# Talking-heads attention and a leaky MLP on one core: raw weight pieces loaded one or two per unit, with four always held

## The chip, the cores and the metric

One core of a Trainium2 chip runs the whole program. The metric is device time in microseconds (us) of one execution; lower is better. Before the change it is 891.46 us (median of 3 runs, 890.16 to 892.83).

## What is computed

```python
# q, k, v: (4, 12, 448, 64); w_pre, w_post: (12, 12)
scores = scale * np.matmul(q, k.transpose(0, 1, 3, 2))
scores = np.einsum('bhij,hg->bgij', scores, w_pre)
attn = np.exp(scores - np.max(scores, axis=-1, keepdims=True))
attn = attn / (np.sum(attn, axis=-1, keepdims=True) + 1e-09)
attn = np.einsum('bhij,hg->bgij', attn, w_post)
x = np.matmul(attn, v)          # then (tokens, 768)
h = x @ w_in                    # w_in: (768, 2048)
g = np.maximum(0.01 * h, h)
out = g @ w_out                 # w_out: (2048, 768)
```

The weights of the MLP arrive as 64-bit numbers, seen as pairs of 32-bit words, and the kernel makes 32-bit floats of them itself.

## The kernel before, in words

**Two phases.** For the first 370 us or so the core computes the attention, for the last 434 us the MLP; some 80 us between them prepare the MLP's operands. The attention is cut into chunks of 120 rows (the last of each batch of 448 has 88), 16 chunks in all, and each chunk `n` into three **units** `s` = 0, 1, 2. A unit has the number `at = 3 * n + s`. The instructions of every engine stand in the order in which the program records them (`pin`, L143), so each engine works through its own list and waits at the first entry that is not ready.

**What a unit does.** For the next unit it mixes the raw scores over the heads: `first` (L218) multiplies the tiles `r` by `kpre` into the PSUM tile `psm`, DVE takes the maxima, ACT the exponentials (`power`, L236, tile `et`). For its own unit it mixes the exponentials back: `mix` (L258), PSUM tile `psa`. `values` (L313, PSUM tile `psx`) multiplies by v for the unit three back. `scores` (L184, PSUM tile `pss`) makes two head pairs of raw scores for the chunk after next, and ACT moves them to the SBUF tile `st` (`move`, L198). `pss`, `psa` and `psx` share a pool of two PSUM buffers (`ps_x`). So an ordinary unit opens on TensorE with a `psm`, and has `psa`, `pss`, `psm`, `pss`, `psa`, `psx` behind it.

**The tiles r.** They are re-reads of `st` in another layout, by DMA: `refill` (L208) issues them on SyncE's queue (SP), four in most units, into a ring of eight tiles, so two units ahead of their use. `st` has two buffers: the first move into a chunk's `st` (the unit with `s` = 0) waits until the DMAs that read the chunk two before have ended.

**The weights.** 48 pieces of the MLP's weights are turned into floats beside the attention, by the class `Narrow` (L74). A piece is loaded raw (L96, `craw`, four buffers, SP's queue), read by ACT into two tiles (`spread`, L102 and L103), put together by DVE (`assemble`) and GpSimd (`join`), and stored to DRAM (L123). The number `count` of pieces that a unit spreads, at its end, is 1, and 2 in the units 5, 11, 17, 23, 29, 35 and 40. The load stands before that, behind the unit's refills:

```python
while len(loaded) < 4 - count and pieces:
    loaded.append(Narrow(p_c, *pieces.pop(0)))
...
for _ in range(count):
    spread()
```

`loaded` holds the pieces that were issued and not yet spread; three are issued ahead of unit 0. Counted out, unit 0 loads none, an ordinary unit one, a unit with `count` = 2 none, and the unit behind it three. All loads of q, k, v (but for some of v), all refills, the raw loads and the stores of pieces share SP's one queue.

Of the kernel before, what the change touches and what calls it, by code (L numbers as in the profile page):

```python
# [34 lines left out]
def kernel(  # L35
# [47 lines left out]
    class Narrow:  # L83
# [14 lines left out]
        def spread(self):  # L98
            self.low, self.high = self.raw[:, :, 0], self.raw[:, :, 1]
            self.w = self.pool.tile([P, PIECE], F32, tag="w", name="w", bufs=self.bufs[1])  # L100
            self.z = self.pool.tile([P, PIECE], F32, tag="z", name="z", bufs=self.bufs[2])
            pin(nc.scalar.activation(self.z, self.high.bitcast(F32), AF.Copy, scale=2.0**-112))  # L102
            pin(nc.scalar.activation(self.w, self.low, AF.Copy, scale=2.0**-52))  # L103

        def assemble(self):
            z = self.z
            self.top = top = self.pool.tile([P, PIECE], U32, tag="top", name="top", bufs=self.bufs[2])
            pin(nc.vector.tensor_scalar(
                top, z.bitcast(U32), 3, 0x7FFFFFF8, op0=ALU.logical_shift_left, op1=ALU.bitwise_and
            ))  # L110
            pin(nc.vector.scalar_tensor_tensor(
                top, z.bitcast(U32), 0x80000000, top, op0=ALU.bitwise_and, op1=ALU.bitwise_or
            ))
            self.exp = z
            pin(nc.vector.tensor_scalar(z.bitcast(U32), top, 0xFF800000, None, op0=ALU.bitwise_and))
# [68 lines left out]
    def scores(n, a, banks=(ps_x, "x")):  # L184
        b, m = chunks[n][0], width(n)
        if a == 0:
            s_t[n] = p_s.tile([CHUNK, H, S], F32, tag="s", name="st")
        pool, tag = banks
        ps = pool.tile([P, 2, 512], F32, tag=tag, name="pss")
        for z in (0, HP):  # L190
            cols = slice(z, min(z + HP, m))
            for e in range(2):
                up = slice(D * e, D * (e + 1))
                mm(ps[cols, e, :S], q_t[n][up, a, cols], k_t[b, a][up], start=True, stop=True)
        return s_t[n][:m, a::NPAIR, :], ps[:m, :, :S]

    def move(to, ps):
        pin(nc.scalar.activation(to, ps, AF.Copy, scale=scale))  # L198
# [9 lines left out]
    def refill(count, *queues):  # L208
        for _, i in zip(range(count), placed):
            n, g = groups[i]  # L210
            m = width(n)
            r_t[n, g] = t = r_all[i % RING]
            pin((queues or (nc.sync, nc.sync))[g % 2].dma_start(  # L213
                t[LOW:LOW + RH], s_t[n][g:m:m // ROWS]
            ))

    def first(n, s, u):

        sg = chunks[n][3][s]
        if u == 0:
            e_t[n, s] = [], p_st.tile([P, 3, NJ], F32, tag="st", name="stat")
        raw = [r_t.pop((n, 2 * sg[u] + b)) for b in range(2)]
        ps = ps_m.tile([P, 2, 512], F32, tag="m", name="psm")
        for b in range(2):
            for y, up in enumerate((slice(0, HP), slice(HP, LOW + RH))):
                mm(ps[HP * b:HP * (b + 1), y, :S], kpre[up], raw[b][up], start=True, stop=True)
        return n, s, u, ps

    def maxima(n, s, u, ps):
        pin(nc.vector.tensor_reduce(  # L232
            e_t[n, s][1][:, 0, 2 * u:2 * u + 2], ps[:, :, :S], axis=AX.X, op=ALU.max, negate=True
        ))

    def power(n, s, u, ps, which=(0, 1)):  # L236
        es, st = e_t[n, s]
        for y in which:
            g = 2 * u + y
            e = p_e.tile([P, S], F32, tag="e", name="et")  # L240
            es.append(e)
            pin(nc.scalar.activation(  # L242
                e, ps[:, y, :S], AF.Exp, bias=st[:, 0, g:g + 1], accum_out=st[:, 1, g:g + 1]
            ))

    def weights(n, s):
        es, st = e_t[n, s]
        kp = p_st.tile([P, NJ, H, ROWS // 2], F32, tag="kp", name="kp")
        kp_t[n, s] = kp
        z = len(es)  # L250
        rs = st[:, 2, :z]
        pin(nc.vector.tensor_scalar_add(rs, st[:, 1, :z], 1e-9))
        pin(nc.vector.reciprocal(rs, rs))
        pin(nc.vector.tensor_mul(
            kp[:, :z].rearrange("p g h x -> p g (h x)"),
            kpost.rearrange("p h x -> p (h x)").unsqueeze(1).broadcast_to([P, z, RH // 2]),
            rs.unsqueeze(2).broadcast_to([P, z, RH // 2]),
        ))  # L258
# [42 lines left out]
    def keep_at(moves):  # L301
        for copy, to, src in moves:
            for_copy(copy, to, src)
# [28 lines left out]
    def keep_x(n, s, ps):  # L332
        m = width(n)
        pin(nc.vector.tensor_copy(  # L334
            xo_t[n][:, RUN * s:RUN * (s + 1), :m].rearrange("p a (x g) -> p a g x", x=ROWS),
            ps[:, :RUN, :m].rearrange("p a (g x) -> p a g x", x=ROWS),
        ))

    def store_x(n):
        b, i0, m, _ = chunks[n]  # L340
        to = x_dram[b][:, NC * i0:NC * (i0 + m)].rearrange("p (c i) -> p c i", c=NC)
        pin(nc.sync.dma_start(to, xo_t.pop(n)[:, :, :m]))
# [220 lines left out]
    def quads_of(n, s):  # L563
        return len(chunks[n][3][s]) if n < NCK else 0
# [13 lines left out]
    pieces = [(f, j) for f in range(NF) for j in range(4)]  # L578
    late_pieces = [(f, j) for f, j in pieces if f >= NF // 2 and j > 1]
    pieces = [piece for piece in pieces if piece not in late_pieces]  # L580
    loaded = [Narrow(p_c, *pieces.pop(0)) for _ in range(3)]
# [28 lines left out]
    def transfers(n, s, c):  # L610
        b = chunks[n][0]
        t = NJ * s + c
        if t == HALF + 1 and n + 3 < NCK:
            load_q(n + 3)
        due = (n % NB - 1) * SLOTS + t - 3
        if b + 1 < B and due % 2 == 0 and 0 <= due < 2 * NPAIR:
            load_k(b + 1, due // 2)
        if n % NB == 0 and n and c == 1 and s:
            load_v(b, s - 1)
        if n % NB == 1 and n > 1 and t == 1:  # L620
            load_v(b, 2)
# [67 lines left out]
    for n in range(NCK):  # L689
        b = chunks[n][0]  # L690
        last = n == NCK - 1
        for s in range(3):
            at = 3 * n + s
            count = (at + 1) * 48 // 41 - at * 48 // 41 if at < 41 else 0
            nxt = (n, s + 1) if s < 2 else (n + 1, 0)
            to, pair = n + 2, 2 * s

            while storing and storing[0][0] < at - (at < 43):
                storing.pop(0)[1].store()
            if at >= 42:  # L700
                end_period(n, s)
                continue

            if kept:
                keep_x(*kept)
            dues = [first(*nxt, 0)] if quads_of(*nxt) else []
            for due in dues:
                maxima(*due)
            refill(2 * len(dues))
            transfers(n, s, 0)  # L710
            if pending:
                keep_at(mix(*pending, 1))
                pending = None
            if to < NCK:
                move(*scores(to, pair))
            transfers(n, s, 1)
            if n > 1 and s == 0:
                store_x(n - 2)
            weights(n, s)

            if quads_of(*nxt) > 1:
                dues.append(first(*nxt, 1))
                maxima(*dues[1])
            if dues:
                power(*dues[0], (0,))
            if to < NCK:
                move(*scores(to, pair + 1))
            refill(2 * len(dues[1:]))
            if dues:
                power(*dues[0], (1,))  # L730
            transfers(n, s, 2)
            while len(loaded) < 4 - count and pieces:
                loaded.append(Narrow(p_c, *pieces.pop(0)))
            keep_at(mix(n, s, 0))
            pending = n, s
            while spreading:
                assemble()
            for due in dues[1:]:
                power(*due)
            for _ in range(count):  # L740
                spread()
            kept = values(n - 1, s) if n else None
            transfers(n, s, 3)
            for piece in joining:
                piece.join()
            storing.extend((at, piece) for piece in joining)
            joining.clear()
# [15 lines left out]
    loaded = []  # L763
# [103 lines left out]
```

## Time and profile before

| what | value |
|---|---|
| median of the runs | 891.46 us |
| time of the profiled execution | 888.53 us |
| its span, first to last instruction | 886.8 us |
| PE matmul busy | 812.8 us (92%) |
| DVE busy | 554.0 us (62%) |
| ACT busy | 510.9 us (58%) |
| GpSimd busy | 137.7 us (16%) |
| mean granted TensorE clock | 0.973 |
| DMA | 150.58 MB, mean 170 GB/s |

The span leaves 1.73 us of the profiled execution's time around it. Busy time is an average over two unlike phases. The MLP keeps TensorE busy nearly without a gap; the attention has gaps on every engine, and what ends them is read from the waits and the timeline of that stretch. The DMA share of a stretch is how busy the 16 DMA engines were in it.

### The profile page before, as it was taken

Reading aid. Unit: us, or ns where it says so; the run is one execution under the profiler, and the core shown is the slowest. Engines: PE = TensorE matmul, PEld = TensorE weight load, DVE = VectorE, ACT = ScalarE, POOL = GpSimd, SP = SyncE. Lnnn points to the kernel's source line nnn. Section 1 sums busy time; section 2 is a strip of 40 time slices with the busy share of each in tenths; the row PEclk is TensorE's granted clock in tenths of the full one; section 3 lists DMA queues with packets and bytes.
Section 4 is the critical chain, followed back from the end, with each engine's and each line's share of the span. In section 5 each row is a group of like instructions: output and inputs, shape, how many; then the busy total and the mean of one; then the engine's idle time right before and its main releaser. Section 6 shows DMA issues by size and latency. Waiting matters only on the chain.

```text
span 886.8 us, 25820 instructions
## 1 busy us (share of the span) xinstructions
PE 812.8 (92%) x10904; PEld 652.2 (74%) x10904; DVE 554.0 (62%) x995; ACT 510.9 (58%) x1000; POOL 137.7 (16%) x161
## 2 busy tenths in 40 slices
PE   8797998978988998958789999999999999999998
PEld 3354665656655665637679999999999999999997
DVE  5477675766857676756876678897645455542443
ACT  3686777756876876744455556574445445443432
POOL 2023245122533225321300000000000000000000
PEclk9899999989999999997999999999999999999999
DMA  6887769776787768563254456526444223221533
GB/s 165 257 256 225 253 200 286 226 227 214 236 257 237 248 208 267 186 198 98 66 186 144 146 152 194 191 87 190 128 124 135 71 72 89 72 72 39 169 109 111
DMA packets 90659, 150.58 MB, mean 170 GB/s; under 512 B 27996, under 2 KB 65584, under 8 KB 90544
## 3 DMA queue, kind: packets, MB, share of 16 engines
q1 hardware_dynamic: 86316, 140.73, 51.5%
q0 software_dynamic: 1680, 4.14, 1.6%
q10 hardware_dynamic: 2548, 4.06, 1.4%
q8 instruction: 86, 1.41, 0.7%
q14 instruction: 29, 0.24, 0.1%
HBM read 85.73 MB, written 23.59 MB: 123 GB/s over the span
## 4 chain that ended last, share of the span: by engine, by line
PE 72%; issue 8%; ACT 7%; DMA 5%; DVE 4%; SPq 2%; POOL 1%; ACTq 0%; POOLq 0%; DVEq 0%
PE pso L148 26%; PE psh L148 22%; PE psx L148 9%; PE psa L148 5%; PE psm L148 5%; PE pss L148 5%; ACT st L198 4%; DMA craw<-in_w_moe 3%; ACT et L242 2%; DVE stat L232 1%; SPq L213 1%; PE idle L148 1%; DMA kt<-in_k 1%; DMA wi<-w_dram 0%; POOL xr L383 0%
## 5 line engine op out<-in xcount | busy, mean ns | idle before, releaser
L148 PEld LDWEIGHTS psa<-kp,et 64*64 64x64 f32 x5888 | 108.6, 140 | 80.9 <-ACT st L198 41.1
L148 PE MATMUL psa<-kp,et 64*64 64x60 f32 (+1 forms) x5888 | 112.4, 224 | 34.2 <-ACT st L198 18.6
L148 PE MATMUL pso<-gh,wl 128*128 128x448 f32 x384 | 140.4, 366 | 0.0
L148 PE MATMUL pso<-gl,wh 128*128 128x448 f32 x384 | 140.3, 365 | 0.0
L148 PE MATMUL pso<-gh,wh 128*128 128x448 f32 x384 | 140.3, 365 | 0.0
L404 DVE TENSOR_TENSOR wl<-wo,wh 128x768 fp32r<-128x768 f32 x64 | 61.2, 956 | 109.0 <-ACT wh L403 108.3
L242 ACT ACTIVATE et<-psm,stat 128x448 f32<-128x448 f32 x184 | 116.1, 640 | 15.7 <-DVE stat L232 15.7
L403 ACT CAST wh<-wo 128x768 fp32r<-128x768 f32 x64 | 53.5, 836 | 121.0 <-PE pso L148 119.8
L232 DVE TENSOR_REDUCE stat<-psm 128x2 f32<-128x896 f32 x92 | 99.5, 1085 | 32.4 <-PE psm L148 32.4
L198 ACT ACTIVATE st<-pss 120x896 f32<-120x896 f32 (+1 forms) x84 | 77.0, 916 | 67.7 <-PE pss L148 52.5
L148 PE MATMUL psm<-r,kpre 64*64 64x448 f32 x736 | 93.7, 567 | 12.3 <-DMA r<-st 9.2
L148 PE MATMUL pss<-kt,qt 64*64 64x448 f32 (+2 forms) x768 | 94.5, 550 | 6.3 <-DMA qt<-in_q 1.8
L119 POOL TENSOR_TENSOR w<-w,z 128x384 f32<-128x384 f32 x48 | 47.9, 999 | 232.3 <-ACT et L242 154.0
L148 PE MATMUL psx<-at,vt 128*64 128x120 f32 (+1 forms) x1152 | 74.4, 282 | 9.6 <-issue 3.5
L148 PEld LDWEIGHTS pso<-gh,wl 128*128 128x128 f32 x384 | 72.1, 188 | 6.4 <-DVE o L519 0.3
L148 PEld LDWEIGHTS pso<-gh,wh 128*128 128x128 f32 x384 | 72.1, 188 | 5.7
L148 PEld LDWEIGHTS pso<-gl,wh 128*128 128x128 f32 x384 | 72.1, 188 | 5.6
L334 DVE COPY xo<-psx 128x240 f32<-128x240 f32 (+1 forms) x48 | 27.2, 568 | 77.4 <-PE psx L148 75.5
L148 PEld LDWEIGHTS psx<-at,vt 128*64 128x64 f32 x1152 | 63.1, 148 | 16.6 <-ACT st L198 9.8
L148 PEld LDWEIGHTS psm<-r,kpre 64*64 64x64 f32 x736 | 25.7, 136 | 40.1 <-issue 26.3
L148 PEld LDWEIGHTS pss<-kt,qt 64*56 64x56 f32 (+2 forms) x768 | 25.1, 129 | 37.7 <-PE pss L148 20.1
L102 ACT ACTIVATE z<-craw 128x384 f32<-128x384 f32 x64 | 36.6, 572 | 23.8 <-DMA craw<-in_w_moe 23.5
(101 smaller groups left out, 1433.6 us busy)
## 6 DMA issues: line engine op xcount, KB each, us to landing
r<-st SPq DMA_DIRECT2D x182, 210.0 KB
craw<-in_w_moe SPq DMA_DIRECT2D x64, 384.0 KB
wo<-w_dram SPq DMA_DIRECT2D x64, 384.0 KB
wi<-w_dram SPq DMA_DIRECT2D x34, 384.0 KB
w_dram<-w SPq DMA_DIRECT2D x64, 192.0 KB
kt<-in_k SPq DMA_DIRECT2D x42, 112.0 KB
x_dram<-xo SPq DMA_DIRECT2D x12, 360.0 KB
xr<-x_dram SPq DMA_DIRECT2D x24, 180.0 KB
```

Source lines behind the costliest of these rows:

```text
L102: pin(nc.scalar.activation(self.z, self.high.bitcast(F32), AF.Copy, scale=2.0**-112))
L119: pin(self.joiner.tensor_mul(w, w, self.exp))
L148: pin(nc.tensor.matmul(*args, **kw))
L198: pin(nc.scalar.activation(to, ps, AF.Copy, scale=scale))
L213: pin((queues or (nc.sync, nc.sync))[g % 2].dma_start(t[LOW:LOW + RH], s_t[n][g:m:m // ROWS]))
L232: pin(nc.vector.tensor_reduce(e_t[n, s][1][:, 0, 2 * u:2 * u + 2], ps[:, :, :S], axis=AX.X, op=ALU.max, negate=True))
L242: pin(nc.scalar.activation(e, ps[:, y, :S], AF.Exp, bias=st[:, 0, g:g + 1], accum_out=st[:, 1, g:g + 1]))
L334: pin(nc.vector.tensor_copy(xo_t[n][:, RUN * s:RUN * (s + 1), :m].rearrange("p a (x g) -> p a g x", x=ROWS), ps[:, :RUN, :m].rearrange("p ...
L403: hold(nc.scalar.copy(hi, raw))
L404: hold(nc.vector.tensor_sub(lo, raw, hi.bitcast(F32)))
```

## The change: what it does

```diff
             transfers(n, s, 2)
-            while len(loaded) < 4 - count and pieces:
+            while len(loaded) < 4 and pieces:
                 loaded.append(Narrow(p_c, *pieces.pop(0)))
             keep_at(mix(n, s, 0))
```

The limit no longer depends on `count`. Unit 0 now loads one piece, a unit with `count` = 2 one, the unit behind it two, and all others one as before. So the first piece of each group of three is issued one unit earlier. The same 64 pieces are loaded, spread and stored. The lists of PE, DVE and ACT keep their order, as does GpSimd's; SP's list is the one that moves.

On SP's list, unit 5 (from its second pair of refills) to unit 6 (its raw loads), before:

```order
L213 DMA r_120<-st 120x1x448
L213 DMA r_121<-st 120x1x448
L156 DMA kt<-in_k 64x448 x2
L123 DMA w_dram_60<-w 128x384
L213 DMA r_122<-st 120x1x448
L213 DMA r_123<-st 120x1x448
L156 DMA kt<-in_k 64x448 x2
L342 DMA x_dram_76<-xo 128x720
L213 DMA r_124<-st 120x1x448
L213 DMA r_125<-st 120x1x448
L96 DMA craw<-in_w_moe 128x768 x3
L123 DMA w_dram_61<-w 128x384
```

and now:

```order
L213 DMA r_120<-st 120x1x448
L213 DMA r_121<-st 120x1x448
L96 DMA craw<-in_w_moe 128x768
L156 DMA kt<-in_k 64x448 x2
L123 DMA w_dram_60<-w 128x384
L213 DMA r_122<-st 120x1x448
L213 DMA r_123<-st 120x1x448
L156 DMA kt<-in_k 64x448 x2
L342 DMA x_dram_76<-xo 128x720
L213 DMA r_124<-st 120x1x448
L213 DMA r_125<-st 120x1x448
L96 DMA craw<-in_w_moe 128x768 x2
```

One raw load has moved from unit 6 into unit 5, ahead of two loads of k, a store and four refills.

On SP's list, units 11 and 12, where a new batch begins, before:

```order
L213 DMA r_118<-st 120x1x448
L213 DMA r_119<-st 120x1x448
L123 DMA w_dram_62<-w 128x384
L213 DMA r_120<-st 120x1x448
L213 DMA r_121<-st 120x1x448
L342 DMA x_dram_76<-xo 128x720
L213 DMA r_122<-st 120x1x448
L213 DMA r_123<-st 120x1x448
L96 DMA craw<-in_w_moe 128x768 x3
```

and now:

```order
L213 DMA r_118<-st 120x1x448
L213 DMA r_119<-st 120x1x448
L96 DMA craw<-in_w_moe 128x768
L123 DMA w_dram_62<-w 128x384
L213 DMA r_120<-st 120x1x448
L213 DMA r_121<-st 120x1x448
L342 DMA x_dram_76<-xo 128x720
L213 DMA r_122<-st 120x1x448
L213 DMA r_123<-st 120x1x448
L96 DMA craw<-in_w_moe 128x768 x2
```

The same move: one of unit 12's three loads stands in unit 11.

On SP's list, units 0 and 1, before:

```order
L213 DMA r_124<-st 120x1x448
L213 DMA r_125<-st 120x1x448
L213 DMA r_118<-st 120x1x448
L213 DMA r_119<-st 120x1x448
L213 DMA r_120<-st 120x1x448
L213 DMA r_121<-st 120x1x448
L96 DMA craw<-in_w_moe 128x768
L167 DMA qt<-in_q 64x6x88 x2
```

and now:

```order
L213 DMA r_124<-st 120x1x448
L213 DMA r_125<-st 120x1x448
L96 DMA craw<-in_w_moe 128x768
L213 DMA r_118<-st 120x1x448
L213 DMA r_119<-st 120x1x448
L213 DMA r_120<-st 120x1x448
L213 DMA r_121<-st 120x1x448
L96 DMA craw<-in_w_moe 128x768
L167 DMA qt<-in_q 64x6x88 x2
```

Unit 0 has a load of its own, ahead of unit 1's four refills and of the loads of q.

## Rows read from the trace of the kernel before

**Rows 1.** Waits, 56 to 374 us: engine, line waited for: us total, times, longest.
```profile
ACT z L102 <- DMA craw<-in_w_moe: 23.4, 6, 6.0
...
ACT st L198 <- DMA r<-st: 4.2, 1, 4.2
```

**Rows 2.** ACT's timeline: start, us, instruction, then [idle before <-what ended it].
```profile
85.75 0.54 ACT L102 ACTIVATE z<-craw 128x384 f32<-128x384 f32 x1 [5.40 <-DMA craw<-in_w_moe]
...
186.32 0.54 ACT L102 ACTIVATE z<-craw 128x384 f32<-128x384 f32 x1 [6.01 <-DMA craw<-in_w_moe]
...
234.48 0.57 ACT L102 ACTIVATE z<-craw 128x384 f32<-128x384 f32 x1 [2.37 <-DMA craw<-in_w_moe]
...
287.59 0.54 ACT L102 ACTIVATE z<-craw 128x384 f32<-128x384 f32 x1 [5.31 <-DMA craw<-in_w_moe]
```

**Rows 3.** SP's timeline, unit 6: the three raw loads.
```profile
80.88 3.40 SPq L96 DMA_DIRECT2D craw<-in_w_moe  x3
```

**Rows 4.** TensorE's timeline: the psm that opens a unit, in five places.
```profile
79.70 0.98 PE L148 MATMUL psm<-r,kpre 64*64 64x448 f32 x8
...
92.26 0.98 PE L148 MATMUL psm<-r,kpre 64*64 64x448 f32 x8
...
99.48 0.98 PE L148 MATMUL psm<-r,kpre 64*64 64x448 f32 x8
...
179.66 0.98 PE L148 MATMUL psm<-r,kpre 64*64 64x448 f32 x8
...
193.72 0.98 PE L148 MATMUL psm<-r,kpre 64*64 64x448 f32 x8
...
231.25 0.98 PE L148 MATMUL psm<-r,kpre 64*64 64x448 f32 x8
...
239.56 0.98 PE L148 MATMUL psm<-r,kpre 64*64 64x448 f32 x8
...
281.63 0.98 PE L148 MATMUL psm<-r,kpre 64*64 64x448 f32 x8
...
293.93 0.98 PE L148 MATMUL psm<-r,kpre 64*64 64x448 f32 x8
```

**Rows 5.** Windows, last columns: granted clock (1.00 is full), DMA share, GB/s.
```profile
116.00:124.00 8.00, 7.44 (x136) 4.86 (x132) 5.67 (x13) 6.57 (x15) 2.00 (x2) 1.00 0.37 138
...
240.00:248.00 8.00, 6.02 (x178) 4.32 (x171) 5.10 (x11) 6.76 (x17) 4.37 (x6) 1.00 1.00 273
...
0.00:374.00 374.00, 326.85 (x7706) 213.23 (x7708) 247.90 (x494) 264.20 (x568) 120.06 (x147) 0.96 0.76 233
```

**Rows 6.** DMA issues of the page: count, KB each.
```profile
craw<-in_w_moe SPq DMA_DIRECT2D x64, 384.0 KB
```

**Rows 7.** TensorE's timeline: idle that nothing in the profile explains ("issue").
```profile
135.33 0.44 PE L148 MATMUL psa<-kp,et 64*64 64x60 f32 x11 [1.09 <-issue]
...
248.25 0.83 PE L148 MATMUL psx<-at,vt 128*64 128x100 f32 x6 [2.14 <-issue]
...
346.78 0.60 PE L148 MATMUL psa<-kp,et 64*64 64x60 f32 x19 [3.38 <-issue]
```

**Rows 8.** Timelines of SP and ACT: unit 8's first refills, unit 9's first move.
```profile
93.84 1.79 SPq L213 DMA_DIRECT2D r<-st  x2
...
102.22 0.92 ACT L198 ACTIVATE st<-pss 120x896 f32<-120x896 f32 x1 [1.17 <-PE pss L148]
```

**Rows 9.** The chain that ended last: start, us, what.
```profile
43.54 3.63 DMA qt<-in_q
...
148.10 2.42 DMA r<-st
```

**Rows 10.** Timelines of ACT and SP, unit 10: spread's end, refills, raw load.
```profile
107.67 0.58 ACT L103 ACTIVATE w<-craw 128x384 f32<-128x384 uint32 x1
...
107.72 1.68 SPq L213 DMA_DIRECT2D r<-st  x2
109.49 0.93 SPq L96 DMA_DIRECT2D craw<-in_w_moe  x1
```

## The prediction

> **What bounds the kernel now.** I read the waits of the attention phase first, because the change touches that phase alone. One wait there names the raw loads: ACT stood idle 23.4 us, six times, until a raw piece had landed [rows 1]. The reader is to see that it is six long waits and not forty short ones. ACT's timeline says where they are [rows 2]: three of 5.40, 6.01 and 5.31 us, and three short ones that make up the rest, 23.4 - 16.7 = 6.7 us. The first stands at the end of unit 6. SP's timeline shows why [rows 3]: the three raw loads of unit 6 begin to be issued at 80.88 us, ACT finishes its other work of the unit at 85.75 - 5.40 = 80.35 us and wants the first of the three at once; it gets it at 85.75 us, 4.9 us after issue. Unit 5 has spread two pieces and loaded none, so unit 6 spreads a piece that it has loaded itself. The same holds behind each unit with `count` = 2, which gives units 6, 12, 18, 24, 30 and 36: six, as the waits say. (Behind unit 40 nothing is left to load.)
>
> The next question is whether ACT's wait is a wait of the kernel. I measure units by the `psm` that opens them on TensorE [rows 4]. An undisturbed unit is 99.48 - 92.26 = 7.22 us. The unit in which ACT waits is 92.26 - 79.70 = 12.56 us, the other two of the long kind 14.06 and 12.30 us. So the path pays: TensorE needs a PSUM buffer that ACT's move of `pss` frees, and that move stands behind the waiting spread in ACT's list. A short wait, at 234.48 us, costs the unit around it 239.56 - 231.25 = 8.31 us, 1.09 us more than an ordinary one.
>
> Last I read the DMA engines, since what is loaded earlier has to find room [rows 5]. Over the attention phase they are busy 0.76 of the time at 233 GB/s. That mean hides both extremes: from 116 to 124 us, where unit 11 runs, the share is 0.37, and from 240 to 248 us, some two units behind a start of a batch, it is 1.00 at 273 GB/s.
>
> **The change, part by part.** Nothing is added or removed; six loads move one unit ahead, and unit 0 gets one. What it does follows from the lists: the piece that unit 6 spreads is loaded in unit 4, two units (14 us) ahead instead of 4.9 us too late.
>
> *The waits removed.* The three long units give 5.34 + 6.84 + 5.08 = 17.3 us over 7.22. For the three short ones the bounds are 0 and ACT's 6.7 us; I take the one pair measured for all three, 3 x 1.1 = 3.3 us. Together **-20.6 us**, at most the 23.4 us that ACT waited.
>
> *What is late next.* Behind a long wait, SP's queue profits from the pause today. In unit 8 the first two refills end their issue at 95.63 us [rows 8], and they are the last reads of a chunk whose buffer unit 9's first move overwrites, at 102.22 us: 6.6 us of room. SP's own work ahead of them is the same number of transfers after the change, while TensorE and ACT come 5.3 us earlier; 1.3 us of room is left. A refill on the chain of waits took 2.42 us from issue to landing [rows 9], so 1.1 us is missing, and with DMA fuller I count 1.7 us. Three times that is 5 us given back. Behind the short waits I take a third of the 3.3 us, 1 us. The bounds are 0 and 10 us, the latter if half of every wait returns; I take **+6 us**.
>
> *The loads moved out of busy stretches.* At the starts of batches (units 12, 24, 36) one load of 384 KB [rows 6] leaves the stretch in which the DMA engines are full and goes into one at 0.37. At 273 GB/s that is 393 KB / 273 = 1.4 us of DMA time, three times 4.3 us. Bounds: 0, and the stalls seen in these stretches: 4.2 us in which a move waited for a refill [rows 1], and 1.09 + 2.14 + 3.38 = 6.6 us in which TensorE stood in the middle of a call with nothing to wait for [rows 7], 10.8 us together. I take **-3 us**, near the 4.3.
>
> The nearest thing to a rule is in the Trainium skill, "Runtime: NRT & Kernel Launch", section "Instruction fetch mechanics": instructions are streamed in blocks by DMA, and the fetch is hidden because a sequencer issues more slowly than the fetch fills. By that, idle inside a call would not come from full DMA engines, the stalls of rows 7 would stay, and the sum would be about 1 to 2 us smaller. The trace has idle of 3.38 us inside one call of 64 alike matmuls, and such idle is longest just where the DMA share is about 1, which speaks for a connection, but does not show it.
>
> *Unit 0's load.* It stands ahead of unit 1's refills and of a load of q that is on the chain of waits for 3.63 us [rows 9]. It costs its issue (0.93 us for one, rows 10) and 1.4 us of DMA time, if both fall on the path: 0 to +2.3 us. I take **+1 us**.
>
> *The loads moved ahead of k.* In units 5, 17 and 29 the raw load now stands ahead of two loads of k and four refills, and delays their issue by up to 0.93 us. The refills are used two units (14 us) later, this k in unit 8. Cost 0; without that cover it is 3 x 0.9 = 2.8 us, which is inside the range.
>
> *Sum.* -20.6 + 6 - 3 + 1 = -16.6 us against the profiled execution's 888.53 us (span 886.8 us), which makes 871.9 us. That execution lies 2.9 us below the median of the runs, so against the median of 891.46 us it is 874.9 us. I predict **875 us**. The MLP phase is not touched and follows as it stands.
>
> **The rivals.**
>
> *A. Most of it is given back.* If the attention phase loses 17 of its 374 us, the same bytes need 233 x 374 / 357 = 244 GB/s on the mean, a share of 0.80. For the rival speaks that stretches are full already. If every refill behind the six places comes late by what the wait had covered, the long ones return 3 us each and the short ones all their 3.3: -20.6 + 12.3 + 1 = -7.3 us, 884 us. Against it speaks that the six loads move towards emptier stretches. The Trainium skill, "DMA: Bandwidth & Descriptors", section "Specifications", gives about 358 GB/s as a core's limit to HBM; by that 244 GB/s would leave much room and the rival would hardly count. The trace speaks against the page here: share 1.00 at 273 GB/s [rows 5], so the room is smaller.
>
> *B. Nothing changes* (within 0.3%, 2.7 us, about what a measurement of this kernel can tell from no change). The raw piece would have hidden another transfer of the same time, one that ACT or TensorE waits for right behind it. For it: the refill waits on the chain. Against it: in unit 7, TensorE's next `psm` ran during ACT's wait, so its refills were there. About 890 us.
>
> *C. Slower: SP is held by ACT.* With four raw buffers and four pieces held, every raw load now needs the buffer that the unit before spread last; before, that buffer had been free for a unit or more. SP would stand at the load until ACT has ended the spread, with refills, q, k and stores behind it. The place where it is tightest is a unit in which the load follows the first two refills: in unit 10 ACT ends its spread at 108.25 us and SP reaches the load at 109.40 us [rows 10], 1.15 us of room; elsewhere SP arrives later, behind four refills. The rival decides from the point at which ACT ends its spread over 1.15 us later against SP than now. If every one of some 37 loads held SP 1 us and the refills had no lead left, it would be -16.6 + 37 = +20 us, 912 us. Against it: the refills have a lead of two units, so that a hold of 1 us is not seen by TensorE.
>
> The Trainium skill, "DMA: Bandwidth & Descriptors", section "Queues, rings and completion order", says that each DMA engine consumes a ring's descriptors in order. By that a raw load's 384 KB stand ahead of whatever SP issues next, also when nothing holds SP; six moved loads of 1.4 us would be 8.4 us at the very most, which leaves rival A's result. The trace shows no wait that would prove or exclude it here.
>
> **How the numbers follow.** My forecast, -10 to -21 us: 0.72. More than that, up to -20.6 - 10.8 + 6 = -25 us: 0.05. Rival A, -3 to -10 us: 0.12. Rival B: 0.07. Rival C: 0.04. The range that leaves out at most 2 in 10 goes from 867 us (-24) to 885 us (-6.5): it holds the forecast and the larger half of A. Faster by over 0.3%: 0.89; within: 0.07; slower: 0.04.
>
> **What would show it.** Right: no wait of ACT for a raw piece behind unit 0's stage, every unit 7, 13, 19, 25, 31 and 37 under 9 us, a first move of units 9, 21 and 33 that waits 1 to 2 us for a refill, a DMA share near 0.80 over a shorter attention phase. A wait of SP's raw loads for ACT with TensorE then waiting for `r` would show C. I am wrong if the six units shrink and others grow by as much, or if ACT still waits for raw pieces.

## The result and the profile after

The changed kernel takes 879.87 us (median of 4 runs, 876.15 to 884.35) against 890.81 us for the kernel before (4 runs, 889.53 to 892.83), timed together: a ratio of 0.990, 95% interval 0.9852 to 0.9948. Timed again later it had 0.9913 (0.9879 to 0.9948). So it is faster by about 0.9%, 7 to 11 us by the medians, where the prediction's sum was 16.6 us. Its profiled execution took 881.49 us (span 879.8), 7.0 us under the profiled one of before; the steps below are read from this pair.

The waits of the changed kernel, 56 to 374 us (engine, line waited for: us in total, times, longest):

```profile
PE psa L148 <- issue: 12.8, 12, 3.0
...
ACT st L198 <- DMA r<-st: 12.5, 4, 4.2
...
PE psx L148 <- issue: 4.1, 3, 1.6
```

ACT's wait for raw pieces, 23.4 us in six waits before [rows 1], has gone from the list. Two others have grown: ACT's moves wait 12.5 us for refills (4.2 before), and TensorE's unexplained idle is longer. The kernel before has these two rows for the latter:

```profile
PE psa L148 <- issue: 7.9, 8, 3.4
...
PE psx L148 <- issue: 3.5, 2, 2.1
```

that is 11.4 us against 16.9 us after.

TensorE's timeline of the changed kernel, the `psm` that open units 7, 8, 9, 10, then 13, 14, then 19, 20, 21, then 31, 32 and 33, which answer to [rows 4]:

```profile
82.45 0.98 PE L148 MATMUL psm<-r,kpre 64*64 64x448 f32 x8
...
89.68 0.98 PE L148 MATMUL psm<-r,kpre 64*64 64x448 f32 x8
...
96.90 0.98 PE L148 MATMUL psm<-r,kpre 64*64 64x448 f32 x8
...
106.36 0.98 PE L148 MATMUL psm<-r,kpre 64*64 64x448 f32 x8
...
127.43 0.98 PE L148 MATMUL psm<-r,kpre 64*64 64x448 f32 x8
...
136.59 0.98 PE L148 MATMUL psm<-r,kpre 64*64 64x448 f32 x8
...
177.76 0.98 PE L148 MATMUL psm<-r,kpre 64*64 64x448 f32 x8
...
184.98 0.98 PE L148 MATMUL psm<-r,kpre 64*64 64x448 f32 x8
...
192.29 0.98 PE L148 MATMUL psm<-r,kpre 64*64 64x448 f32 x8
...
275.52 0.98 PE L148 MATMUL psm<-r,kpre 64*64 64x448 f32 x8
...
283.29 0.98 PE L148 MATMUL psm<-r,kpre 64*64 64x448 f32 x8
...
292.63 0.98 PE L148 MATMUL psm<-r,kpre 64*64 64x448 f32 x8
```

The three long units, 12.56, 14.06 and 12.30 us before, are now 7.23, 7.22 and 7.77 us. Unit 13, one of the short waits, is as long as ever: 136.59 - 127.43 = 9.16 us. And unit 9, an ordinary one of 7.23 us before, has grown to 106.36 - 96.90 = 9.46 us. ACT's timeline says what it waits for:

```profile
101.95 0.92 ACT L198 ACTIVATE st<-pss 120x896 f32<-120x896 f32 x1 [3.51 <-DMA r<-st]
```

This is unit 9's first move, which waited 1.17 us for TensorE before [rows 8].

The long units have a second part that the waits do not name: the clock that TensorE was granted. The end of unit 7 on TensorE, before:

```profile
87.59 1.88 PE L148 MATMUL psa<-kp,et 64*64 64x60 f32 x64 [3.71 <-ACT st L198]
89.40 2.29 PE L148 MATMUL psx<-at,vt 128*64 128x120 f32 x24
```

in a window whose last columns are granted clock, DMA share and GB/s:

```profile
88.00:91.00 3.00, 3.00 (x72) 2.89 (x67) 0.00 (x0) 3.00 (x9) 1.88 (x2) 0.50 0.67 251
```

and after:

```profile
86.44 1.11 PE L148 MATMUL psa<-kp,et 64*64 64x60 f32 x64
87.66 1.45 PE L148 MATMUL psx<-at,vt 128*64 128x120 f32 x24
```

Before, TensorE stood 3.71 us for ACT's move and then ran the same matmuls at clock 0.50, the lower of its two levels (1.2 GHz), in 1.88 and 2.29 us instead of 1.11 and 1.45 us. So of the 5.3 us that unit 7 was too long, 3.9 us lie ahead of this `psa` and 1.4 us behind it; in units 19 and 31 it is 4.5 and 2.3, 3.8 and 1.3 us. Over the stretch from the opening of unit 4 to that of unit 41, before and then after, the windows have (first the length, TensorE's busy time and its matmuls):

```profile
56.38:365.96 309.58, 274.30 (x6741) 185.06 (x6740) 210.35 (x422) 223.57 (x483) 104.77 (x116) 0.96 0.77 237
```

```profile
59.33:357.47 298.14, 267.25 (x6741) 180.03 (x6740) 210.18 (x422) 224.07 (x483) 104.92 (x116) 0.99 0.80 244
```

The stretch is 11.4 us shorter. 7.0 us of that are TensorE's busy time for the same 6741 matmuls, at a mean clock of 0.99 instead of 0.96, and 4.4 us are idle time. The program opens unit 4 2.95 us later and takes 1.5 us longer behind unit 41's opening, which leaves the 7.0 us of the pair. This is an account of two traces; no experiment held the clock fixed.

The windows (granted clock, DMA share, GB/s at the end) show that the load did move into the slack of unit 11: from 116 to 124 us the share was 0.37 [rows 5]. At 242 instead of 138 GB/s these 8 us carry 0.83 MB more, of which the load is 0.39 MB; the rest is other traffic that now falls into the same stretch.

```profile
116.00:124.00 8.00, 7.42 (x140) 4.29 (x136) 5.99 (x16) 7.47 (x17) 2.01 (x2) 1.00 0.71 242
```

Two windows of the changed kernel give the rest: behind the start of the next batch the engines are as full as ever, and the phase as a whole is at 0.79 (0.76 before).

```profile
232.00:240.00 8.00, 5.71 (x143) 4.11 (x137) 4.51 (x10) 6.16 (x14) 3.86 (x5) 1.00 1.00 250
...
0.00:360.00 360.00, 313.37 (x7548) 205.01 (x7552) 242.61 (x483) 259.25 (x557) 118.44 (x145) 0.99 0.79 239
```

### The profile page after: what moved, and what is told of

The parts are those of the page before. It is cut to its first block, busy times and chain, and to the rows that moved or that the text cites. A ratio compares the mean times of both kernels' runs of the same rounds, so it can differ in the third digit from the quotient of the medians.

```text
span 879.8 us, 25843 instructions
## 1 busy us (share of the span) xinstructions
PE 806.6 (92%) x10904; PEld 648.2 (74%) x10904; DVE 554.3 (63%) x995; ACT 511.0 (58%) x1000; POOL 137.9 (16%) x161
## 3 DMA queue, kind: packets, MB, share of 16 engines
q8 instruction: 86, 1.41, 0.7%
## 4 chain that ended last, share of the span: by engine, by line
PE 71%; issue 9%; ACT 6%; DMA 6%; DVE 5%; SPq 2%; POOL 1%; POOLq 0%; DVEq 0%; ACTq 0%
PE pso L148 27%; PE psh L148 22%; PE psx L148 8%; PE psm L148 5%; PE pss L148 5%; PE psa L148 4%; ACT st L198 3%; DMA r<-st 3%; ACT et L242 2%; DMA craw<-in_w_moe 2%; DVE stat L232 1%; DVE top L111 1%; PE idle L148 1%; SPq L213 1%; POOL xr L383 0%
## 5 line engine op out<-in xcount | busy, mean ns | idle before, releaser
L148 PEld LDWEIGHTS psa<-kp,et 64*64 64x64 f32 x5888 | 108.5, 139 | 78.7 <-issue 35.5
L148 PE MATMUL psa<-kp,et 64*64 64x60 f32 (+1 forms) x5888 | 112.1, 222 | 32.8 <-issue 13.4
L148 PE MATMUL pso<-gh,wl 128*128 128x448 f32 x384 | 141.1, 367 | 0.0
L148 PE MATMUL pso<-gh,wh 128*128 128x448 f32 x384 | 140.9, 367 | 0.0
L148 PE MATMUL pso<-gl,wh 128*128 128x448 f32 x384 | 140.9, 367 | 0.0
L198 ACT ACTIVATE st<-pss 120x896 f32<-120x896 f32 (+1 forms) x84 | 77.1, 918 | 83.1 <-PE pss L148 55.3
L148 PE MATMUL psm<-r,kpre 64*64 64x448 f32 x736 | 92.0, 558 | 13.0 <-DMA r<-st 10.3
L148 PE MATMUL pss<-kt,qt 64*56 64x448 f32 (+2 forms) x768 | 94.9, 545 | 7.0 <-DMA qt<-in_q 2.1
L148 PE MATMUL psx<-at,vt 128*64 128x120 f32 (+1 forms) x1152 | 70.0, 272 | 8.5 <-ACT st L198 3.0
L148 PEld LDWEIGHTS pso<-gh,wl 128*128 128x128 f32 x384 | 72.1, 188 | 7.1 <-DVE o L519 0.3
L148 PEld LDWEIGHTS pso<-gl,wh 128*128 128x128 f32 x384 | 72.1, 188 | 6.7
L148 PEld LDWEIGHTS pso<-gh,wh 128*128 128x128 f32 x384 | 72.1, 188 | 6.6
L148 PEld LDWEIGHTS psx<-at,vt 128*64 128x64 f32 x1152 | 59.0, 141 | 15.2 <-ACT st L198 10.4
L148 PEld LDWEIGHTS psm<-r,kpre 64*64 64x64 f32 x736 | 25.7, 134 | 39.2 <-issue 24.2
L148 PEld LDWEIGHTS pss<-kt,qt 64*56 64x56 f32 (+2 forms) x768 | 25.9, 128 | 37.5 <-PE pss L148 19.7
L309 ACT COPY at<-psa 128x960 f32<-128x960 f32 x44 | 43.1, 980 | 12.3 <-PE psa L148 12.3
```

The source lines that it names most:

```text
L148: pin(nc.tensor.matmul(*args, **kw))
L309: pin(copy(to, src))
```

## The experiments

Each group of runs was timed beside the kernel before on one chip; ratios are to that kernel, with their 95% intervals. The groups ran on different chips, so ratios are compared and not microseconds.

**Where the gain sits: long waits or short ones.** The edit of the kernel before is one line, in two versions:

```diff
-            while len(loaded) < 4 - count and pieces:
+            while len(loaded) < 4 - (1 if at in (5, 17, 29) else count) and pieces:    # long only
+            while len(loaded) < 4 - (1 if at in (11, 23, 35) else count) and pieces:   # short only
```

> The kernel before with one load moved from units 6, 18 and 30 into 5, 17 and 29 only, so that the three long waits go and the three short ones stay. My theory: nearly all of the gain is here, since the long units shrink by 5 to 7 us each and the short ones hardly did: 6 to 10 us under the kernel before. Rival, the loads moved out of busy stretches at the starts of batches carry the gain: under 4 us.

> The kernel before with one load moved from units 12, 24 and 36 into 11, 23 and 35 only; the three long waits stay. My theory: the DMA engines are full behind these units, ACT's wait is replaced by others there, and units 13, 25 and 37 gain 0.8 us in all: 0 to 2 us under the kernel before. Rival of my prediction's own sum (three waits of 1.1 us and 1.4 us of DMA time each): 5 to 7 us under it.

Long only: 878.26 against 887.91 us, 0.9890 (0.9854 to 0.9926). Short only: 887.52 us, 0.9981 (0.9953 to 1.0009). Three moved loads carry the whole gain, and the other three carry none that can be measured: the interval ends at 4.2 us, under the 5.3 us that the prediction's sum gave them (3.3 less 1 given back, and 3). The long waits stay where they were left, as ACT's timeline of short only has them:

```profile
86.48 0.55 ACT L102 ACTIVATE z<-craw 128x384 f32<-128x384 f32 x1 [6.93 <-DMA craw<-in_w_moe]
...
188.41 0.54 ACT L102 ACTIVATE z<-craw 128x384 f32<-128x384 f32 x1 [6.11 <-DMA craw<-in_w_moe]
...
287.96 0.54 ACT L102 ACTIVATE z<-craw 128x384 f32<-128x384 f32 x1 [5.31 <-DMA craw<-in_w_moe]
```

The pair also shows the price behind the long wait. Units 9 and 10 open on TensorE, long only:

```profile
93.14 0.98 PE L148 MATMUL psm<-r,kpre 64*64 64x448 f32 x8
...
103.46 0.98 PE L148 MATMUL psm<-r,kpre 64*64 64x448 f32 x8
```

and short only:

```profile
101.40 0.98 PE L148 MATMUL psm<-r,kpre 64*64 64x448 f32 x8
...
108.62 0.98 PE L148 MATMUL psm<-r,kpre 64*64 64x448 f32 x8
```

Where the long wait is gone unit 9 takes 10.32 us, where it stands 7.22 us: 3.1 us come back two units later, behind a first move that waits 4.36 us for refills. Unit 33 grows likewise, 9.71 against 7.22 us, but what its first move waits for the profile doesn't name. Unit 21 grows too, 10.31 against 7.37 us; there TensorE stands 1.05 and 1.76 us in unexplained idle, and not for the move.

**Three held instead of four, and unit 0's load.** Two kernels that differ from the changed one and from the one before in one number each:

```diff
-            while len(loaded) < 4 and pieces:                                # the changed kernel
+            while len(loaded) < 3 and pieces:                                # three held
-            while len(loaded) < 4 - count and pieces:                        # the kernel before
+            while len(loaded) < 4 - (0 if at == 0 else count) and pieces:    # start only
```

> Three pieces held in every unit instead of four; unit 0 loads none, a unit with count = 2 loads one. My theory: the six waits of ACT are gone as after the change (each of those pieces is issued one unit, some 8 us, before its use, and landed in 4.9 us), and unit 0's extra load, behind which unit 4 opened 2.95 us later (59.33 against 56.38 us), costs nothing: some 877 us (874 to 880). Rival, that it takes four held pieces: ACT still waits in units 6, 12, 18, 24, 30 and 36, and the time is 883 to 888 us.

> Three pieces held, again, as the base of this group: 10 to 12 us under the kernel before if the first figure (875.7 against 887.1 us) holds, 7 us if three and four held are the same.

> The kernel before with one load moved from unit 1 into unit 0 and nothing else. My theory: the load of unit 0 delays unit 1's refills and with them a move of unit 3, 2 to 3 us, with all six waits for raw pieces as before: 893 to 894 us. Rival, the late start after the change had another cause: 891 us, unit 4 opens at 56.4 us as before.

Three held: 875.70 against 887.12 us, 0.9884 (0.9850 to 0.9919), and in another group 878.16 against 890.00 us, 0.9879 (0.9852 to 0.9907). Three pieces are enough; both figures lie under the changed kernel's 0.990 and 0.9913, though the intervals overlap. Start only: 893.27 against 887.12 us, 1.0055 (1.0027 to 1.0083), slower by about 5 us. In this kernel unit 1 then loads none, so that one load has moved ahead by a unit. So the load in unit 0 does cost here; how much of it the changed kernel pays no run shows by itself, and three held, which goes without it, is only 1 to 3 us faster by the ratios. Where it costs is not shown: its one profiled execution was the fastest of its runs, and its unit 4 opens at 57.01 us. Nor does the late unit 4 of the changed kernel prove it, for in the second run of three held, without that load, it opens as late:

```profile
59.64 0.98 PE L148 MATMUL psm<-r,kpre 64*64 64x448 f32 x8
```

My place for this cost fell; the size, from the timed runs, stands.

**SP held by ACT.** The changed kernel with `bufs=(5, 5, 3)` for `Narrow` instead of `(4, 5, 3)`:

> The changed kernel with five raw buffers instead of four, so that a raw load on SP's queue no longer waits for the spread of the unit before. My theory: that wait costs nothing, 880 us (877 to 882), units as long as after the change. Rival, SP held by ACT returns part of the gain: moves wait less for refills than the 12.5 us after the change, and the time is 875 us or less.

881.52 against 887.12 us, 0.9943 (0.9915 to 0.9970): not faster than with four buffers. Moves still wait 11.6 us for refills in its trace. So a fifth buffer buys nothing. It doesn't settle the wait of SP's raw loads for ACT as a cause, because SP's own waits have raw loads standing for ACT as long as after the change (12.0 us in both, 5.9 us before).

**The changed kernel again.**

> The changed kernel once more, beside the others of this group on one chip, to compare it with three held pieces and with each half of the gain. 9 to 11 us under the kernel before, as when it was first timed, if the first figure (890.81 to 879.87 us) was typical; 6 us, as five buffers gave, if four or five buffers make no difference and that figure was lucky.

880.82 against 887.91 us, 0.9913 (0.9879 to 0.9948): between the two figures I had named, so the first was a little lucky at most. Its runs spread from 874.98 to 885.26 us, more than 1%.

**Half the bytes.** The raw tile keeps half its columns, and the spread reads them twice, so the kernel leaves out the other half of these weights:

```diff
+            n = PIECE // 2 if self.half else PIECE
+            at = slice(PIECE * j, PIECE * j + n)
...
+                high, low = (t.unsqueeze(1).broadcast_to([P, 2, PIECE // 2]) for t in (high, low))
```

> The changed kernel with half the bytes in each of the 48 raw loads beside the attention (192 KB instead of 384 KB); the spread reads the half twice, so ACT, DVE and GpSimd do the same work. This leaves out half of the weights' columns of those pieces. My theory, that a fuller DMA returns part of the gain: TensorE's idle inside its calls, 17.5 us after the change and 11.3 before, falls below 11 us, moves wait under 4 us for refills instead of 12.5, and the time is some 868 us (864 to 873). Rival, that this idle has nothing to do with DMA: it stays near 17 us, and the time is 875 to 880 us.

862.88 against 887.12 us, 0.9739 (0.9695 to 0.9783). Its waits, 56 to 374 us (L205 and L155 are L198 and L148 of the others):

```profile
ACT st L205 <- DMA r<-st: 9.9, 3, 4.1
PE psa L155 <- issue: 5.1, 8, 1.7
PE psx L155 <- issue: 3.2, 2, 1.9
...
PE psm L155 <- issue: 0.3, 1, 0.3
```

The unexplained idle fell to 8.6 us as expected, the waits for refills only from 12.5 to 9.9 us, not under 4. The time fell by some 15 us beyond the changed kernel: with the waits for raw pieces gone, the phase still pays for the amount of data moved beside it. By which of the waits it pays is not shown.

**The raw loads on GpSimd's queue.**

```diff
-            pin(nc.sync.dma_start(self.raw..., w_moe[f, :, at].bitcast(U32)))
+            pin(joiner.dma_start(self.raw..., w_moe[f, :, at].bitcast(U32)))   # joiner is nc.gpsimd for these
```

> The changed kernel with the 48 raw loads issued from GpSimd's queue instead of SP's, so that SP's refills stand behind no raw load. My theory, that what is full are the DMA engines and not SP's queue: moves still wait for refills about as long (12 to 17 us) and the time is within 3 us of the changed kernel. Rival, SP's queue is what makes the refills late: those waits fall under 5 us and the time is 4 to 8 us lower. If GpSimd's issue holds up its joins, it could be slower without telling either.

889.89 against 887.91 us, 1.0012 (0.9984 to 1.0040): the whole gain is gone. Its waits, 56 to 374 us:

```profile
POOL craw L96 <- ACT w L103: 26.4, 29, 2.7
...
PE psa L148 <- issue: 12.8, 12, 2.8
...
PE psx L148 <- issue: 8.0, 4, 2.9
PE psm L148 <- issue: 4.1, 2, 2.6
...
ACT st L198 <- DMA r<-st: 2.5, 1, 2.5
```

The moves hardly wait for refills any more, which is what the rival said: refills are late because they stand behind raw loads on SP's queue. But TensorE's unexplained idle is now 24.9 us and GpSimd stands 26.4 us for ACT. From the opening of unit 4 to that of unit 41 the run takes 310.82 us, 12.7 us more than the changed kernel, and 10.9 us of these are TensorE's busy time (278.12 against 267.25 us) at a mean clock of 0.96. The run speaks for SP's order as the cause of those waits and against this way of mending it; which of its new waits brings the loss was not tested.

**Taking transfers from ahead of the refills.** All on top of three held:

```diff
-            while len(loaded) < 3 and pieces:
+            while len(loaded) < (2 if at in (7, 19, 31) else 3) and pieces:    # skip seven
...
-            while storing and storing[0][0] < at - (at < 43):                  # store behind:
-                storing.pop(0)[1].store()                                      # from the unit's top
...
                 loaded.append(Narrow(p_c, *pieces.pop(0)))
+            while storing and storing[0][0] < at - (at < 43):                  # to behind the raw loads
+                storing.pop(0)[1].store()
```

> Three pieces held, but units 7, 19 and 31 load none and units 8, 20 and 32 two, so that the raw load that stands ahead of unit 8's refills goes behind them; no other transfer moves. My theory: the first move of units 9, 21 and 33 waits for those refills, which a raw load (0.6 us of issue and 1.4 us of DMA time) made later; each of these units comes under 8 us more often, and the time is 2 to 4 us under plain three held. Rival, that the raw load is not what makes them late (the pause of ACT had let SP catch up with everything): no change against plain three held.

> Three pieces held, and the stores of finished pieces issued behind a unit's refills and raw load instead of ahead of them; nothing else moves. Same theory, other transfer: unit 8's refills lose one store ahead of them (0.5 us of issue, 192 KB), all other units too, and the moves wait less for refills: 1 to 3 us under plain three held. Rival: a store then stands ahead of the next unit's loads of q and refills, and nothing is gained.

> Three pieces held, no raw load in units 7, 19 and 31, and stores issued behind the refills: the two edits that each came out a little under plain three held. My theory, that both take transfers from ahead of the same refills: at least as fast as the better of the two, 13 to 17 us under the kernel before. Rival, that the difference between them and plain three held is the spread between runs: 11 to 13 us under it.

Skip seven: 875.48 against 890.00 us, 0.9852 (0.9828 to 0.9875). Store behind: 877.25 us, 0.9837 (0.9799 to 0.9875). Plain three held in the same group: 0.9879 (0.9852 to 0.9907). Both came out lower, with overlapping intervals. Both edits together: 872.91 against 888.64 us, 0.9819 (0.9779 to 0.9859), the best of the kernels that leave nothing out. Its interval is clear of the changed kernel's second figure (0.9879 to 0.9948), not of its first nor of plain three held. (In the last units the stores stay where they stood.) The mechanism is only half seen. With skip seven alone, unit 8's first refills were issued at the same moment as after the change, because the loads of q ahead of them took longer; SP's timeline of skip seven and then of the changed kernel:

```profile
96.10 4.54 SPq L213 DMA_DIRECT2D r<-st  x4
```

```profile
96.14 4.09 SPq L213 DMA_DIRECT2D r<-st  x4
```

and unit 9 still took 106.20 - 96.24 = 9.96 us. With both edits these refills are issued at 93.10 us, and unit 9 takes 8.68 us; but it took 8.40 and 10.83 us in the two traces of plain three held, so one trace each can't show the edits at work.

## Why the prediction was right, and where its sizes were off

The direction, the place and the mechanism held; the time lay in the range. But by the ratios the change gives 8.9 and 7.7 us, which lies in rival A's band of -3 to -10 us and not the forecast's -10 to -21: the range holds it because it was drawn to take in the larger half of A. Of the signs named ahead, two were missed: unit 13 stayed over 9 us (9.16), and unit 33's first move waited for no refill. The step that was sized wrong is the third of the sum, "the loads moved out of busy stretches", and with it the short waits in the first; the load of unit 0 may have been under-sized.

- *The waits removed* (-20.6). Right for the long ones: 16.7 us of the 17.3 came off the three units. The prediction read all of it as the path through ACT's wait; some 5 us of the 17.3 were matmuls at clock 0.50 behind the wait, a part that a price by unit length takes in without naming it. Wrong for the short ones: I took 3.3 us, and the units of that kind gave 0.8 us in all (9.10 to 9.16, 8.31 to 7.82, 8.18 to 7.82); short only, timed, gave 0.4 us with an interval that holds zero. The base of 7.22 us was wrong there: without any such wait units 25 and 37 still take 7.82 us.
- *What is late next* (+6). Right in kind and place: unit 9's first move waits 3.51 us for the refills that SP issues behind the former pause, and the unit grows by 2.2 us; 3.1 us in long only. Units 21 and 33, where I expected the same, grew by 0.1 and 0 us after the change, though unit 21's first move waited 2.04 us for refills; in long only unit 33 grew by 2.5 us. So this term measured 2 to 6 us.
- *The loads moved out of busy stretches* (-3). This failed. The load went into the slack, as the window shows (0.37 to 0.71), but nothing was gained for it: short only contains exactly these three moves and is even with the kernel before. The idle inside TensorE's calls, which I had hoped to shrink, grew from 11.4 to 16.9 us. Nor is it longest where the DMA engines are full, as I had read it: in the 3.4 us ahead of the longest, at 346.78 us before, the DMA share was 0.73. I had priced a stretch by its DMA time, as if the path there followed the DMA engines; the runs showed that one load less leaves it as long.
- *Unit 0's load* (+1). Start only measured about 5 us; its place is open, and so is what it costs in the changed kernel. I had counted one load's own issue and transfer.
- *The loads ahead of k* (0). No sign of a cost: moves wait 3.5 us for k in two waits after the change, 3.6 us before.
- *The rivals.* A, most given back, was nearer than I had it: the result lies in its band by the ratios and at its edge by the first pair of medians. The 273 GB/s at a share of 1.00, from which A's room was read, is no fixed ceiling: from 133.0 to 134.2 us the same trace carries 385 GB/s, so it depends on the mix of transfers. C, slower because SP is held by ACT, fell with the result itself, and a fifth buffer bought nothing.

With the measured sizes the sum is -17.5 (waits) + 2 to 6 (refills) + about 5 (unit 0) + 0 = -6 to -10 us, against 7.0 us in the pair of profiles and 7 to 11 us by the medians. The terms come from different kernels and executions, so that they meet the result is no proof of each.

What stays open is how much of the rest is TensorE's unexplained idle. It differs between two executions of the same kernel (16.9 and 13.9 us for the changed one), so one trace each doesn't settle it.

## What to carry to other kernels

When a load's consumer waits, look whether the load was issued in the same stage: a prefetch limit that shrinks just when more will be used leaves the next stage without stock, and keeping one stage ahead is enough; a deeper stock bought nothing here. Then ask what used the pause: transfers on the same queue had caught up during it, and come late when it goes. Price a removed wait by the span between fixed points of the bounding engine, not by the waiting engine's idle time, expect little of it where the DMA engines are full, and look at the granted clock behind the wait: part of what the wait cost here was matmuls at half clock.

## What the runs showed of the hardware that I had not expected

**The clock.** In the attention phase of the kernel before, TensorE's granted clock fell to 0.50 six times, 23.9 us in all between 56 and 374 us; after the change once, for 3.4 us. Each of the six falls came during an idle stretch of TensorE or right behind one; these stretches had lasted 2.1 to 4.3 us, and three of them are the waits of the long units. Not every long stretch has a fall: the 2.59 us below were followed by none.

**The unexplained idle.** It falls at places fixed by the program, though not each of them shows in every execution. The piece of a call behind it has the same count before and after the change at several of them, 11, 18, 19 or 25 matmuls, while its length differs: 1.09 and 1.20 us before the one with 11, 3.38 and 3.03 us before the one with 19 [rows 7]. Before one with 18 it grew from 0.16 to 2.59 us; TensorE's timeline of the kernel before and of the changed one:

```profile
259.86 0.48 PE L148 MATMUL psa<-kp,et 64*64 64x30 f32 x18 [0.16 <-issue]
```

```profile
253.65 0.48 PE L148 MATMUL psa<-kp,et 64*64 64x30 f32 x18 [2.59 <-issue]
```

Counted in TensorE's instruction list (weight loads, matmuls and its semaphore instructions), all 159 such idles between 56 and 374 us of the 14 traces stand 192 to 195 instructions behind a multiple of 256. So they stand at one place in blocks of 256 instructions. The profile's list of DMA queues has one for instructions:

```profile
q8 instruction: 86, 1.41, 0.7%
```

1.41 MB in 86 packets is 16.4 KB each, and TensorE's 2 x 10904 instructions in 86 packets are 254 each, 256 with the semaphore instructions. The Trainium skill, "Runtime: NRT & Kernel Launch", section "Instruction fetch mechanics", has the fetch in blocks of 16 KiB, or 256 instructions, and calls the cost of crossing a block's boundary mostly hidden. The sizes agree with the Trainium skill there; idle of up to 3.4 us once per block is not hidden. That TensorE waits there for the fetch itself, and what makes it late at one boundary and not at another, is my inference, not shown.
